# Weights on a second DMA queue, and larger first blocks, in a retention and FFN kernel

## Chip, cores and metric

The kernel runs on one core of one Trainium2 chip. Times are device microseconds (us) of one execution. The kernel before took 227.93 us (median of 3 runs, 227.45 to 228.94). The profiles show one execution each, and their span is some 2 us shorter than the run's time.

Ratios are the mean time of one kernel's fast runs over that of the other's fast runs of the same rounds on the same chip, so they are not quite the ratio of the medians that are quoted beside them. Their intervals are 95% intervals.

## The reference

```python
B, H, S, D = 4, 8, 768, 64                      # q, k, v: float32
gamma = 1.0 - 2.0 ** (-5.0 - np.arange(H))
state = zeros((B, H, D, D))
for t in range(S):                              # retention: linear attention with a decay
    state = gamma * state + einsum('bhd,bhe->bhde', k[:, :, t], v[:, :, t])
    y[:, :, t] = 1/sqrt(D) * einsum('bhd,bhde->bhe', q[:, :, t], state)
x = y.transpose(0, 2, 1, 3).reshape(3072, 512)
h = np.maximum(x @ w_in, 0.0)                   # w_in 512 x 2048
out = h * h @ w_out                             # w_out 2048 x 512
```

## The kernel before

The 3072 tokens are cut into 24 chunks of 128. For each chunk the kernel loads keys, queries and values (256 KB each), casts them, flips keys and queries on TensorE (the timeline's matmuls against `ident`), and does the attention of the chunk in "visits" (the small 64x64 matmuls). The FFN follows: product 1 (`F1`, with `w_in`), relu on ScalarE, square on VectorE, product 2 (`F2`, with `w_out`). Matmuls are in bf16; all inputs come as float32 and are cast on the chip by VectorE, ScalarE or GpSimd.

A list scheduler in Python fixes the order of every engine's instructions when the program is built. It uses assumed durations (the constants below). At run time each engine works through its list strictly in order; semaphores only make it wait.

Loads come in three kinds. The first chunks' keys and queries come as *pairs*: two chunks in one load, in rows of 4 KB. Other chunks, and all values, come in rows of 256 bytes. The weights come in eight loads of 1 MB in rows of 2 KB: `w_in` quarters 0 to 3, `w_out` quarters 0 to 3. Everything is issued by SyncE, on one queue, in the order of `ORDER` (p a pair, i and o quarters of `w_in` and `w_out`).

```python
SMALL = (1.20, 1.55, 65)       # us of queue time assumed for a chunk's load
PAIR = (1.4, 1.6, 9)
WIDE = (2.75, 2.75, 33)        # a quarter of a weight
BLOCKS = [1, 1, 2, 2, 2, 4, 4, 4, 4]   # chunks that share one pass of product 1
WARM = 10.0                    # until then idle time of TensorE is filled with dummy matmuls ("fillers")
NFP = 3                        # pairs
ORDER = "p0 i0 p1 i1 i2 i3 o0 p2 o1 o2 o3"
# ... cut ...
# a pair of keys or queries, and a chunk's values:
nc.sync.dma_start(ld[x][:, slot : slot + 2, :].rearrange("s u n -> s (u n)"),
                  src[x][b : b + 2, :, i * C : (i + 1) * C, :].rearrange("b h (w t) d -> (b h) w (t d)", t=16))
nc.sync.dma_start(t.rearrange("s (h d) -> s h d", h=H),
                  src[x][b, :, i * C : (i + 1) * C, :].rearrange("h s d -> s h d"))
# ... cut ...
def weights(kind, j):
    slot = (j if kind == "in" else 4 + j) % NWS          # one of NWS staging buffers
    # ...
    pl.add(f"ldw{kind}{j}", "SP", WIDE, (), (f"wst{slot}",),
           lambda: nc.sync.dma_start(st[:], wv), prio=dma_prio[(kind, j)])
    for c in range(4):   # casts, by whichever engine the scheduler picks
        pl.add(f"cw{kind}{j}.{c}", WCAST, 0, (f"wst{slot}",), (f"w{kind}{j}.{c}",), ...)
# ... cut ...
def ffn1(blk):
    n = blocks[blk] * C          # 128, 256 or 512 columns
    reads = [f"xt{g % NXT}.{u0 + u}" for u in range(blocks[blk])] + ...   # all chunks of the block
    # 16 feature blocks x 4 matmuls of 128 x n, then relu (ScalarE) and square (VectorE)
```

A block of n chunks costs 64 matmuls of 128·n columns in product 1, and it can start only when all its n chunks are through the attention.

Of the kernel before, what the change touches and what calls it, by code (L numbers as in the profile page):

```python
# [18 lines left out]
class Plan:  # L19
# [6 lines left out]
    DMA_LATENCY = 1.9  # L26
    LAND = 1.25
    RING = 198
    FETCH = 2.6
    BLOCK0 = 193  # L30
    BLOCK = 256
# [32 lines left out]
    def schedule(self, nbanks, max_open):  # L64
        ops = self.ops
        n = len(ops)
        users = [[] for _ in range(n)]
        left = [len(o["deps"]) for o in ops]
        for o in ops:
            for d in o["deps"]:  # L70
                users[d].append(o["i"])
        ready_at = [0.0] * n
        start = [None] * n
        end = [None] * n
        eng_free = {}
        pool = {}
        for o in ops:
            for e in o["eng"]:
                eng_free.setdefault(e, 0.0)
                pool.setdefault(e, set())  # L80
                if left[o["i"]] == 0:
                    pool[e].add(o["i"])
        bank_free = [0.0] * (nbanks - 1) + [WARM]
        bank_of = {}
        open_groups = set()
        shared = [0.0, 0.0]
        outstanding = {e: [] for e in eng_free}
        done = 0
        issued, edge, next_fetched, history, crossed = 0, self.BLOCK0, 3.0, [], 0.0
        while done < n:  # L90
            best = None
            for eng, cand in pool.items():
                ef = eng_free[eng]
                for i in cand:
                    o = ops[i]
                    t = max(ef, ready_at[i])
                    b = o["bank"]
                    if b is not None and b[0] == "open":
                        if b[2] and len(open_groups) >= max_open:
                            continue  # L100
                        free = [x for x in bank_free if x is not None]
                        if not free:
                            continue
                        t = max(t, min(free))
                    key = (t, o["prio"], i)
                    if best is None or key < best[0]:
                        best = (key, i, eng)
            assert best is not None, "no operation can be placed"
            (t, _, _), i, eng = best
            o = ops[i]  # L110
            for e in o["eng"]:
                pool[e].discard(i)
            o["on"] = eng
            dur = o["eng"][eng]
            move = isinstance(dur, tuple)
            if move:
                out_ = outstanding[eng]
                while out_ and out_[0][0] <= t:
                    out_.pop(0)
                while sum(x[1] for x in out_) + dur[2] > self.RING:  # L120
                    t = max(t, out_.pop(0)[0])
            start[i] = t
            b = o["bank"]
            if b is not None and b[0] == "open":
                k = min((x, j) for j, x in enumerate(bank_free) if x is not None)[1]
                bank_free[k] = None
                bank_of[b[1]] = k
                if b[2]:
                    open_groups.add(b[1])
            if move:  # L130
                dur, n_desc = (dur[:2] if t < 50 else dur[:1] * 2), dur[2]
                eng_free[eng] = t + 0.08
                for w in range(2):
                    shared[w] = max(shared[w], t + self.DMA_LATENCY) + dur[w]
                end[i] = max(shared) + self.LAND
                out_.append((max(shared), n_desc))
                dur = 0.08
            else:
                if eng == "PE":
                    o["fill"] = 0  # L140
                    if t < WARM:
                        o["fill"] = int(max(0.0, t - max(eng_free[eng], 1.5) - 0.3) * FILL / 0.213)
                    issued += 2 * o["fill"]
                    todo, per = 2 * o["count"], dur / max(1, 2 * o["count"])
                    now = t
                    while issued + todo > edge:
                        step = max(0, edge - issued)
                        now = max(now + step * per, next_fetched)
                        issued, todo = max(issued, edge), todo - step
                        ahead = next((y for x, y in reversed(history) if x <= edge - self.AHEAD), 0.0)  # L150
                        ahead = max(ahead, crossed)
                        crossed = now
                        edge += self.BLOCK
                        next_fetched = ahead + min(5.7, max(0.3, max(shared) - ahead)) + self.FETCH
                    issued += todo
                    dur = now + todo * per - t
                    history.append((issued, t + dur))
                    o["dur"] = dur
                eng_free[eng] = t + dur
                end[i] = t + dur + o["lat"]  # L160
            if b is not None and b[0] == "close":
                bank_free[bank_of[b[1]]] = end[i]
                open_groups.discard(b[1])
            if b is not None:
                o["bank_index"] = bank_of[b[1]]
            done += 1
            for u in users[i]:
                same = list(ops[u]["eng"]) == [eng] and not move
                ready_at[u] = max(ready_at[u], start[i] + dur if same else end[i] + self.HOP)
                left[u] -= 1  # L170
                if left[u] == 0:
                    for e in ops[u]["eng"]:
                        pool[e].add(u)
        self.start, self.end, self.on = start, end, [o["on"] for o in ops]
        return sorted(range(n), key=lambda i: (start[i], i))


SMALL = (1.20, 1.55, 65)
PAIR = (1.4, 1.6, 9)
WIDE = (2.75, 2.75, 33)  # L180
STORE = (0.72, 0.72, 9)
BLOCKS = [1, 1, 2, 2, 2, 4, 4, 4, 4]
SPLIT = 6
WARM = 10.0
FILL = 0.8
PACE = 6
LEAD = 7
NFP = 3
F2LAG = 5.0
F2WAIT = 4  # L190
CAST = {"k": {"DVE": 0.43, "ACT": 0.63, "POOL": 0.78}, "q": {"DVE": 0.43, "ACT": 0.63, "POOL": 0.78}}
# [2 lines left out]
WPRIO = {"in": -2.0, "out": 2.0}  # L194


ORDER = "p0 i0 p1 i1 i2 i3 o0 p2 o1 o2 o3"


def dma_order(nm):  # L200
# [13 lines left out]
def kernel(  # L214
# [9 lines left out]
    nc = tc.nc  # L224
    P = nc.NUM_PARTITIONS
# [14 lines left out]

    blocks = BLOCKS
    assert sum(blocks) == NM
    NB = len(blocks)
    blk0 = [sum(blocks[:i]) for i in range(NB)]
    for x, n in zip(blk0, blocks):
        assert 512 % (n * C) == 0 and x // 4 == (x + n - 1) // 4
    NLD, NBF, NQT, NXT, NH2, NWS, NOSB, NST = 4, 4, 4, 4, 3, 4, 3, 4
    NBANK = 4

    const = ctx.enter_context(tc.tile_pool(name="const", bufs=1))  # L250
# [5 lines left out]
    ident = sb("ident", [P, P], BF16)  # L256
# [17 lines left out]
    wst = [sb(f"wst{j}", [P, 4, 512], FP32) for j in range(NWS)]  # L274
# [5 lines left out]
    fps = [psum.tile([P, 512], FP32, name=f"fps{j}") for j in range(NBANK)]  # L280
# [3 lines left out]
    pl = Plan()  # L284
# [63 lines left out]
    def prepare(m):  # L348
        b, i = where(m)
        slot = m % NLD  # L350
        for x in "kqv":
            t = ld[x][:, slot, :]
            if x != "v" and m < 2 * NFP:
                if m % 2 == 0:
                    pl.add(f"ld{x}{m}", "SP", PAIR, (), (f"ld{x}{slot}", f"ld{x}{slot + 1}"),
                           lambda x=x: nc.sync.dma_start(  # L356
# [206 lines left out]
    def weights(kind, j):  # L563
        slot = (j if kind == "in" else 4 + j) % NWS
        st = wst[slot]
        dst = w_in_bf[j] if kind == "in" else w_out_bf[j]
        wv = (moe_w_in.rearrange("(cb p) f -> p cb f", p=P)[:, :, j * 512 : (j + 1) * 512] if kind == "in"
              else moe_w_out.rearrange("(fb p) n -> p fb n", p=P)[:, 4 * j : 4 * j + 4, :])
        pl.add(f"ldw{kind}{j}", "SP", WIDE, (), (f"wst{slot}",),
               lambda: nc.sync.dma_start(st[:], wv), prio=dma_prio[(kind, j)])  # L570
        for c in range(4):
            pl.add(f"cw{kind}{j}.{c}", WCAST, 0, (f"wst{slot}",), (f"w{kind}{j}.{c}",),
                   lambda on, c=c: copy_on(on, dst[:, c, :], st[:, c, :]),
                   prio=WPRIO[kind] + j)
# [71 lines left out]
    dma_prio = {x: n for n, x in enumerate(dma_order(NM))}  # L646
# [6 lines left out]
    for m in range(-1, NM):  # L653
# [18 lines left out]
        else:  # L672
            if n == SPLIT:
                transpose(n)
            t = n + 1 if n + 1 < NM else None
# [13 lines left out]
    if tc is not None:  # L689
        with tc.manual_schedule():  # L690
            for i in sequence:
                o = pl.ops[i]
                for _ in range(o.get("fill", 0)):
                    nc.tensor.matmul(fps[NBANK - 1][:, 0 : 2 * P], lhsT=ident[:],
                                     rhs=ident[:, None, :].to_broadcast([P, 2, P]), start=True, stop=True)
                o["fn"](o["on"]) if o["flex"] else o["fn"]()
    return pl

# [29 lines left out]
```

## Time and profile before

| what | number | where it is read |
|---|---|---|
| span, mean granted TensorE clock | 224.9 us, 1.000 | cores |
| TensorE busy from 0 to 40 us | 28.4 of 40 | busy time by stretch |
| TensorE busy from 40 to 90 us | 48.0 of 50 | busy time by stretch |
| TensorE busy from 90 to 221 us | 130.9 of 131 | busy time by stretch |
| first matmul of product 1 | 15.93 us | timeline |

So TensorE is full from about 41 us on, and before that it waits for its inputs. These are lines of the first page of the kernel before: the busy tenths of TensorE, its granted clock and the DMA rate in 40 slices of 5.6 us, and the chain of work that ended last.

```profile
PE   5667878889999998999999999999999999999993
PEclk9999999999999999999999999999999999999999
GB/s 138 246 272 291 382 304 187 366 258 210 273 212 192 226 209 185 234 211 202 203 239 197 51 50 3 47 50 23 24 47 50 47 47 1 47 50 47 93 49 91
...
PE 78%; DMA 11%; SPq 5%; issue 2%; ACT 2%; DVE 1%; POOL 1%; ACTq 0%; POOLq 0%
```

TensorE is 50% to 80% busy in its first slices and then full. The clock row reads 9 throughout, but for its first four slices it is not to be trusted: the trace has no clock record before 23.4 us, and the matmuls show half the pace until then (below). The last chain spends 16% of the span in loads (DMA) and in SyncE's queue (SPq), nearly all of it in the start.

The timeline of TensorE and of SyncE's issues in the kernel before, with start, duration, engine, line, operation and, in brackets, the idle time ahead and what ended it:

```profile
9.54 0.61 PE L422 MATMUL fps<-ident,qkT 128*128 128x128 bf16 x4
15.93 1.33 PE L594 MATMUL fps<-xt,w_in 128*128 128x128 bf16 x11 [1.22 <-DVE xt L556]
25.30 2.13 PE L594 MATMUL fps<-xt,w_in 128*128 128x128 bf16 x31 [0.73 <-DVE w_in L343]
...
2.09 1.21 SPq L363 DMA_DIRECT2D vn<-in_v_dram  x2
3.34 4.84 SPq L570 DMA_DIRECT2D wst<-in_moe_w_in_dram  x1
8.22 0.55 SPq L356 DMA_DIRECT2D kn<-in_k_dram  x1
```

The first pair's keys are flipped back at 9.5 us, and product 1 of chunk 0 starts at 15.9 us. Counted from the starts of the matmuls, those of 128 columns follow one another every 106 to 107 ns before 23.4 us and every 56 ns after it.

### The profile page before, as it was taken

Reading aid. Unit: us, or ns where it says so; the run is one execution under the profiler, and the core shown is the slowest. Engines: PE = TensorE matmul, PEld = TensorE weight load, DVE = VectorE, ACT = ScalarE, POOL = GpSimd, SP = SyncE. Lnnn points to the kernel's source line nnn. Section 1 sums busy time; section 2 is a strip of 40 time slices with the busy share of each in tenths; the row PEclk is TensorE's granted clock in tenths of the full one; section 3 lists DMA queues with packets and bytes.
Section 4 is the critical chain, followed back from the end, with each engine's and each line's share of the span. In section 5 each row is a group of like instructions: output and inputs, shape, how many; then the busy total and the mean of one; then the engine's idle time right before and its main releaser. Section 6 shows DMA issues by size and latency. Waiting matters only on the chain.

```text
span 224.9 us, 7277 instructions
## 1 busy us (share of the span) xinstructions
PE 207.4 (92%) x3242; PEld 118.3 (53%) x3242; DVE 116.0 (52%) x251; ACT 105.4 (47%) x167; POOL 40.1 (18%) x65
## 2 busy tenths in 40 slices
PE   5667878889999998999999999999999999999993
PEld 3547766744577874455555554444444444444441
DVE  1496878772189985899887754422222222230000
ACT  8233626853357763576545564344435444343121
POOL 3221225234233322324323100000000000000000
PEclk9999999999999999999999999999999999999999
DMA  6999999999999998999998110110011110111212
GB/s 138 246 272 291 382 304 187 366 258 210 273 212 192 226 209 185 234 211 202 203 239 197 51 50 3 47 50 23 24 47 50 47 47 1 47 50 47 93 49 91
DMA packets 70975, 34.02 MB, mean 151 GB/s; under 512 B 63008, under 2 KB 63008, under 8 KB 70944
## 3 DMA queue, kind: packets, MB, share of 16 engines
q1 hardware_dynamic: 70944, 33.56, 59.3%
q8 instruction: 25, 0.41, 0.8%
q14 instruction: 6, 0.05, 0.1%
HBM read 27.26 MB, written 6.29 MB: 149 GB/s over the span
## 4 chain that ended last, share of the span: by engine, by line
PE 78%; DMA 11%; SPq 5%; issue 2%; ACT 2%; DVE 1%; POOL 1%; ACTq 0%; POOLq 0%
PE fps L632 35%; PE fps L594 33%; DMA qn<-in_q_dram 11%; PE yy L390 3%; SPq L570 2%; SPq L356 2%; PE yy L469 2%; PE sc L480 1%; ACT qkT L437 1%; PE yy L454 1%; PE sc L491 1%; DVE xt L556 1%; POOL qs L345 1%; SPq L363 1%; PE yy L403 0%
## 5 line engine op out<-in xcount | busy, mean ns | idle before, releaser
L594 PE MATMUL fps<-xt,w_in 128*128 128x512 bf16 (+2 forms) x576 | 96.9, 313 | 2.2 <-DVE xt L556 1.2
L632 PE MATMUL fps<-w_out,h 128*128 128x512 bf16 x384 | 92.9, 379 | 0.0
L599 ACT ACTIVATE h<-fps 128x512 bf16<-128x512 f32 x96 | 57.1, 596 | 58.2 <-PE fps L594 58.1
L604 DVE TENSOR_TENSOR h<-h 128x512 bf16<-128x512 bf16 x96 | 44.3, 476 | 49.9 <-ACT h L599 49.8
L594 PEld LDWEIGHTS <-w_in 128*128 128x128 bf16 x576 | 51.1, 100 | 34.3 <-issue 1.8
L632 PEld LDWEIGHTS <-h 128*128 128x128 bf16 x384 | 36.9, 98 | 43.3
L640 ACT ACTIVATE osb<-fps 128x512 f32<-128x512 f32 x24 | 14.3, 597 | 26.9 <-PE fps L632 26.9
L556 DVE TENSOR_TENSOR xt<-yy,yf 128x512 bf16<-128x512 f32 x24 | 16.5, 689 | 18.8 <-ACT qkT L437 16.2
L437 ACT ACTIVATE qkT<-yy 128x1024 bf16<-128x1024 bf16 x18 | 18.4, 1024 | 11.5 <-PE yy L469 10.3
L345 POOL CAST ks<-kn 128x512 bf16<-128x512 f32 x21 | 15.2, 725 | 35.8 <-DMA kn<-in_k_dram 25.0
L378 DVE TENSOR_TENSOR vs<-vn,vf 128x512 bf16<-128x512 f32 x24 | 17.8, 741 | 4.9 <-DMA vn<-in_v_dram 4.9
L345 POOL CAST qs<-qn 128x512 bf16<-128x512 f32 x21 | 14.1, 673 | 22.8 <-DMA qn<-in_q_dram 22.6
L547 DVE TENSOR_TENSOR state<-sc,state 128x256 bf16<-128x256 f32 x40 | 16.7, 418 | 0.5
L534 DVE TENSOR_TENSOR pt<-sc,cmask 128x512 bf16<-128x512 f32 x24 | 16.3, 681 | 0.8 <-PE sc L491 0.8
L469 PE MATMUL yy<-qkT,state 64*64 64x64 bf16 x352 | 12.3, 200 | 0.4
L454 PE MATMUL yy<-pt,vs 64*64 64x64 bf16 x384 | 7.8, 198 | 2.2 <-issue 1.4
L480 PE MATMUL sc<-qkT 64*64 64x64 bf16 x384 | 8.2, 198 | 1.5 <-issue 1.5
L469 PEld LDWEIGHTS <-state 64*64 64x64 bf16 x352 | 7.6, 107 | 1.2 <-PE yy L469 1.2
L491 PE MATMUL sc<-vs,ks 64*64 64x64 bf16 x352 | 7.7, 197 | 0.0
L454 PEld LDWEIGHTS <-vs 64*64 64x64 bf16 x384 | 5.5, 110 | 3.9 <-issue 2.8
L345 POOL CAST w_out<-wst 128x512 bf16<-128x512 f32 x7 | 5.3, 781 | 11.7 <-DMA wst<-in_moe_w_out_dram 11.7
L390 PEld LDWEIGHTS <-ks 64*64 64x64 bf16 x288 | 3.7, 107 | 6.8 <-issue 6.6
(46 smaller groups left out, 87.4 us busy)
## 6 DMA issues: line engine op xcount, KB each, us to landing
vn<-in_v_dram SPq DMA_DIRECT2D x24, 256.0 KB, 5.5
out_dram<-osb SPq DMA_DIRECT2D x24, 256.0 KB, 2.0
kn<-in_k_dram SPq DMA_DIRECT2D x18, 256.0 KB, 5.2
qn<-in_q_dram SPq DMA_DIRECT2D x18, 256.0 KB, 5.4
wst<-in_moe_w_in_dram SPq DMA_DIRECT2D x4, 1024.0 KB, 10.8
wst<-in_moe_w_out_dram SPq DMA_DIRECT2D x4, 1024.0 KB, 13.0
kn<-in_k_dram SPq DMA_DIRECT2D x3, 512.0 KB, 8.0
qn<-in_q_dram SPq DMA_DIRECT2D x3, 512.0 KB, 10.1
```

What stands on the lines that cost most here:

```text
L345: nc.gpsimd.tensor_copy(o, t)
L378: lambda: nc.vector.tensor_tensor(out=o[:], in0=t.rearrange("s (h d) -> s h d", h=H), in1=vf[:, i, :, None].to_broadcast([P, H, D]), op=AL ...
L437: lambda: nc.scalar.activation(qkT.rearrange("p x j (s t) -> p s (x j) t", s=2), tpv.rearrange("p s (g t) -> p s g t", t=L), AF.Copy), pri ...
L454: nc.tensor.matmul(yy[L * c : L * c + L, sub, p * L : p * L + L], lhsT=vs[r, 4 * a + j, :], rhs=pt[r, a, j, :], start=(p == 0), stop=True, ...
L469: nc.tensor.matmul(yy[L * c : L * c + L, sub, p * L : p * L + L], lhsT=st[r, j, :], rhs=qkT[r, 1, j, sub * L : sub * L + L], start=False, ...
L534: lambda: nc.vector.tensor_tensor(out=pt[:], in0=sc[:, :, 0:256].rearrange("s g (p t) -> s g p t", p=NJ), in1=cmask[:, None, None, :].to_b ...
L547: f = lambda cc=cc, j1=j1, j0=j0: nc.vector.tensor_tensor(out=sts[j1][:], in0=cc, in1=sts[j0][:], op=ALU.add)
L556: lambda: nc.vector.tensor_tensor(out=xt[:, :, u * C : u * C + C].rearrange("s p (g t) -> s g p t", g=2), in0=yy[:, :, 0:256].rearrange("s ...
L594: nc.tensor.matmul(ps[:, u * n : u * n + n], lhsT=w_in_bf[j][:, cb, c * P : (c + 1) * P], rhs=xt[:, cb, cols], start=(cb == 0), stop=(cb = ...
L599: nc.scalar.activation(h2[:, f0 : f0 + per, cols], ps[:].rearrange("p (u n) -> p u n", u=per), AF.Relu)
L604: nc.vector.tensor_mul(hv, hv, hv)
L632: nc.tensor.matmul(ps[:], lhsT=h2[:, fb, u * C : u * C + C], rhs=w_out_bf[j][:, c, :], start=(fb == 0), stop=(fb == NFB - 1))
```

## The change

The intent is to let weights and chunks load side by side, so that more bytes are moved early, and to save matmuls of product 1 with larger first blocks. The core of the diff:

```diff
+    MIX = {"SP": 1.25, "ACT": 1.8}       # how much slower each queue is assumed to run beside the other
@@ the scheduler's model of the loads: one shared clock becomes one per queue
-                for w in range(2):
-                    shared[w] = max(shared[w], t + self.DMA_LATENCY) + dur[w]
+                mine, other = shared[eng], max(shared[e] for e in shared if e != eng)
+                begin, slow = max(mine, t + self.DMA_LATENCY), self.MIX[eng]
+                both = max(0.0, min(other - begin, dur[1] * slow))
+                shared[eng] = begin + both + max(0.0, dur[1] - both / slow)
@@ constants
-PAIR = (1.4, 1.6, 9)
+PAIR = (2.4, 2.4, 9)
-BLOCKS = [1, 1, 2, 2, 2, 4, 4, 4, 4]
-SPLIT = 6
-WARM = 10.0
+BLOCKS = [2, 2, 4, 4, 4, 4, 4]
+SPLIT = 4
+WARM = 20.0
-LEAD = 7
-NFP = 3
+LEAD = 5
+NFP = 2
-ORDER = "p0 i0 p1 i1 i2 i3 o0 p2 o1 o2 o3"
+ORDER = "p0 p1 i0 i1 i2 i3 o0 o1 o2 o3"
@@ staging buffers of the weights: NWS 4 -> 3; fillers of 512 columns in place of 256
@@ weights
-        pl.add(f"ldw{kind}{j}", "SP", WIDE, (), (f"wst{slot}",),
-               lambda: nc.sync.dma_start(st[:], wv), prio=dma_prio[(kind, j)])
+        pl.add(f"ldw{kind}{j}", "ACT", WIDE, (), (f"wst{slot}",),
+               lambda: nc.scalar.dma_start(st[:], wv), prio=-150 + dma_prio[(kind, j)])
```

More of the change, by code (lines that the diff above doesn't have):

```diff
@@ L85, in schedule @@
         open_groups = set()
-        shared = [0.0, 0.0]
+        shared = {"SP": 0.0, "ACT": 0.0}
         outstanding = {e: [] for e in eng_free}
@@ L132, in schedule @@
                 eng_free[eng] = t + 0.08
-                for w in range(2):
-                    shared[w] = max(shared[w], t + self.DMA_LATENCY) + dur[w]
-                end[i] = max(shared) + self.LAND
-                out_.append((max(shared), n_desc))
+                mine, other = shared[eng], max(shared[e] for e in shared if e != eng)
+                begin, slow = max(mine, t + self.DMA_LATENCY), self.MIX[eng]
+                both = max(0.0, min(other - begin, dur[1] * slow))
+                shared[eng] = begin + both + max(0.0, dur[1] - both / slow)
+                end[i] = shared[eng] + self.LAND
+                out_.append((shared[eng], n_desc))
                 dur = 0.08
@@ L141, in schedule @@
                     if t < WARM:
-                        o["fill"] = int(max(0.0, t - max(eng_free[eng], 1.5) - 0.3) * FILL / 0.213)
+                        o["fill"] = int(max(0.0, t - max(eng_free[eng], 1.5) - 0.3) * FILL / 0.427)
                     issued += 2 * o["fill"]
@@ L153, in schedule @@
                         edge += self.BLOCK
-                        next_fetched = ahead + min(5.7, max(0.3, max(shared) - ahead)) + self.FETCH
+                        next_fetched = ahead + min(5.7, max(0.3, max(shared.values()) - ahead)) + self.FETCH
                     issued += todo
@@ L246 @@
         assert 512 % (n * C) == 0 and x // 4 == (x + n - 1) // 4
-    NLD, NBF, NQT, NXT, NH2, NWS, NOSB, NST = 4, 4, 4, 4, 3, 4, 3, 4
+    NLD, NBF, NQT, NXT, NH2, NWS, NOSB, NST = 4, 4, 4, 4, 3, 3, 3, 4
     NBANK = 4
@@ L693 @@
                 for _ in range(o.get("fill", 0)):
-                    nc.tensor.matmul(fps[NBANK - 1][:, 0 : 2 * P], lhsT=ident[:],
-                                     rhs=ident[:, None, :].to_broadcast([P, 2, P]), start=True, stop=True)
+                    nc.tensor.matmul(fps[NBANK - 1][:], lhsT=ident[:],
+                                     rhs=ident[:, None, :].to_broadcast([P, 4, P]), start=True, stop=True)
                 o["fn"](o["on"]) if o["flex"] else o["fn"]()
```

## The prediction

> **What bounds the kernel now.** Two regimes. From 90 to 221 us TensorE is busy 130.9 of 131 us (busy time by stretch). From 40 to 90 us it is busy 48.0 of 50. Before 41 us it lacks inputs: the chain of waits runs through loads (DMA of q 11% of the span, SyncE's queue 5%). The timeline shows the one queue's order: first key pair usable at 6.4 us, its values 10.6, w_in quarter 0 at 14.1, second pair's q 18.9, third pair's q 37.8, and the last quarter of w_out at 50.0. TensorE's first FFN matmul starts at 15.9. Rates over 2 us stretches: weights 384 to 399 GB/s, 4 KB pairs and 256-byte rows only 170 to 250.
>
> **What changes.**
> 1. Weights go on ScalarE's queue. The Trainium skill ("DMA: Bandwidth & Descriptors", "Issuing engines are not separate DMA queues") says that both share 16 engines and only issue time is saved; this trace, with one load queue, cannot show it. As pairs and chunks draw half the weights' rate, I expect the mixture to move more (estimate 300 to 350 GB/s against 10.2 MB in the first 39.4 us, 259 GB/s, now). Chunk loads then run about a quarter slower than alone, weights nearly twice as slow. Estimate: w_out complete at 42 to 46 us (was 50), chunks 4 to 7 landed at 45 to 50 (was 56.8).
> 2. One pair less: some 2 us more queue time, hidden.
> 3. Blocks. The matmul count of the first product drops from 576 to 448. From the timeline, 128 columns cost 77 ns, 256 cost 115, 512 cost 216: 128x77 + 192x115 + 256x216 = 87.2 us becomes 128x115 + 320x216 = 83.8 us, so 3.4 us less TensorE work. But the first FFN matmul waits for two chunks and, by the order of instructions, for the flips of the second pair: it starts later, near 20 us (15.9 before).
> 4. ScalarE gives about 0.55 us (SyncE's figure) to each of eight issues: small.
> 5. Fillers: 16 of 512 instead of 18 of 256 columns: little.
>
> **Sum.** Dense TensorE work left from the point where it is no longer starved, which by the new order is the arrival of chunk 7, about 46 us: 16x115 ns + 320x216 + 376x216 of the FFN, 17 visits of 0.93 = 168 us, plus 1.5 us of stalls and 3.65 us of tail: span about 219. The same sum for before (178 us from 41.0, plus 2.2) gives the observed 221.3. Median runs are 3 us over the profiled span.
>
> **Prediction: 221 us**, 8 in 10 between 213 and 229. Faster by over 2%: 0.62; within 2%: 0.29; slower: 0.09.
>
> **What shows it right or wrong.** Stretches: 0 to 40 us moves 300 GB/s or more (step 1), w_out lands before 46. First FFN matmul near 20 us, and TensorE dense from about 46 us with at most 2 us idle afterwards. In the chain the share of DMA falls.
>
> **What would make it wrong.** If mixing gives no more bytes, chunk 7 lands near 57 us as now, and the time is 229 or more. If the weights' 2 KB rows crowd out the values' 256-byte rows, the first visits slip past 17 us. "Issue" pauses of TensorE (three of 0.8 to 1.4 us before 48 us now) could grow with two full queues. If mixing is better than I estimate, dense work starts by 40 us and the time nears 214.

## The result

The changed kernel takes 236.05 us (median of 4, 234.89 to 236.58) beside 227.82 us (median of 4) of the kernel before in the same rounds: a ratio of 1.0346, interval 1.029 to 1.0402. It is 3.5% slower. Executions over 1.5% slower than the fastest of the same kernel are left out of the means. The prediction was 221 us.

The same lines of the changed kernel's page; a slice is 5.9 us here:

```profile
PE   5205879489999999999999999999999999999993
PEclk9655559859999999999999999999999999999998
GB/s 215 261 337 221 333 341 311 268 207 226 177 204 207 202 197 170 182 223 215 181 243 92 47 0 47 47 47 0 47 45 46 20 28 45 45 45 47 89 45 89
...
PE 76%; DMA 18%; issue 1%; SPq 1%; ACT 1%; POOL 1%; DVE 0%; POOLq 0%; ACTq 0%
```

The third slice of TensorE is 0: it does nothing in these 5.9 us, which lie within a wait of 9.1 us (below). By the trace's clock records its clock had fallen to half before that, at 7.8 us, in a first idle time of 4.1 us. It stays there until 35.1 us, and falls once more from 45.4 to 52.2 us. In the kernel before the half pace ended at 23.4 us. The Trainium skill ("TensorE: Matmul & The Clock Gate", "Part 1: The HAM clock gate") says that an idle TensorE drops to half its clock and that busy time brings it back. This trace agrees: eight matmuls of 256 columns take 1.89 us at 32.3 us, where the clock row reads 5, and 1.05 us at 43.9 us. The loads' share of the last chain rose from 11% to 18%. The rate row shows that the change did move more bytes early (mean of 0 to 40 us, by stretches: 262 GB/s before, 288 after), which was its intent.

How much of product 1 was done by when? Busy time of the lines of product 1 alone, by stretch: start and end, length, TensorE busy and number of matmuls, weight loads of TensorE, and for all engines together the clock, the DMA share and GB/s. First the kernel before, then the changed one:

```profile
0.00:40.00 40.00, 12.57 (x152) 10.90 (x152) 1.00 1.02 262
40.00:50.00 10.00, 4.70 (x40) 3.77 (x40) 1.00 1.02 323
```

```profile
0.00:40.00 40.00, 5.87 (x41) 4.20 (x42) 0.66 1.04 288
40.00:50.00 10.00, 2.94 (x24) 2.16 (x24) 0.77 1.05 252
```

Until 50 us the changed kernel has done 65 matmuls of 256 columns, which is one chunk pair's 64 and one more. The kernel before has done 192 matmuls, 128 of 128 columns and 64 of 256: four chunks. The loss is there: after 50 us TensorE is busy for another 178.3 us in the changed kernel and for 170.2 us in the kernel before, and these 8.1 us are most of the 9.9 us between the two spans. Later the two kernels work alike: from 90 us to its last matmul TensorE is idle for 0.1 us in the kernel before and for 1.0 us in the changed one.

Why did the start slip? The timelines of the changed kernel, first TensorE, then ScalarE, then SyncE's issues:

```profile
9.16 1.11 PE L406 MATMUL sc<-ident,ks 128*64 128x64 bf16 x32 [4.08 <-DVE ks L346]
10.21 0.61 PE L697 MATMUL fps<-ident 128*128 128x512 bf16 x1
19.91 1.03 PE L425 MATMUL fps<-ident,qkT 128*128 128x128 bf16 x8 [9.10 <-ACT qkT L344]
...
32.34 1.89 PE L597 MATMUL fps<-xt,w_in 128*128 128x256 bf16 x8
...
7.65 1.15 ACT L344 ACTIVATE w_in<-wst 128x512 bf16<-128x512 f32 x2 [0.50 <-DMA wst<-in_moe_w_in_dram]
18.84 0.37 ACTq L573 DMA_DIRECT2D wst<-in_moe_w_in_dram  x1
19.26 0.60 ACT L344 ACTIVATE qkT<-sc 128x512 bf16<-128x512 f32 x1 [10.46 <-DMA vn<-in_v_dram]
...
2.09 3.90 SPq L366 DMA_DIRECT2D vn<-in_v_dram  x2
6.03 7.49 SPq L359 DMA_DIRECT2D kn<-in_k_dram  x1
```

The keys of the first pair are flipped at 9.2 to 10.3 us. Half of the result waits on ScalarE for its evacuation from PSUM (`qkT<-sc`), and ScalarE does this only at 19.26 us. Ahead of it in ScalarE's list stands the issue of the fourth weight load. That issue itself takes 0.37 us, but it started at 18.84. The bracket says what ended the idle time: the landing of a *value* load, which is SyncE's and has nothing to do with the weights. TensorE stood for 9.1 us. Even then product 1 started only at 32.3 us, since the second pair and the values had come late as well.

When did the loads land? Counted from the landing events of the trace, in us:

```
                    pair 0: k    q     v0     v1  | pair 1: k    q     v2     v3 | w_in0 w_in3 w_out3
before                   6.4   8.5   9.6   10.7  |        16.3  18.9  19.8   20.9 | 14.1  29.7  50.0
after                    8.7  11.7  17.5   18.7  |        21.0  23.2  24.4   25.5 |  7.6  29.6  45.4
```

The values of the first pair came 8 us later than before. The last of the weights came 4.6 us earlier. The weights won, the chunks lost.

### How the two queues shared the engines

This table is counted from the DMA records of the changed kernel's trace. q1 is SyncE's queue, q10 ScalarE's; "rows" are the records of one size that ended in the 2 us stretch, on all 16 DMA engines; the last column of each queue is the mean time of one row.

```
stretch      q1, 256-byte rows             q10, 2 KB rows
12 to 14 us   321 rows,  41 GB/s, 19 ns     306 rows, 313 GB/s, 93 ns
30 to 32 us   322 rows,  41 GB/s, 19 ns     308 rows, 315 GB/s, 93 ns
48 to 50 us  1644 rows, 210 GB/s, 20 ns     none
22 to 24 us, kernel before (one queue)      368 rows, 377 GB/s, 88 ns
```

The numbers of rows are nearly equal. Equal numbers would also come of longer turns of equal length, so the order of the records was looked at (they don't name the engine). From 12 to 14 us each 256-byte row has on average 1.15 ends of 2 KB rows 4 or 5 ns after its start, where chance gives 0.3. Each 2 KB row has 1.25 ends of 256-byte rows 3 or 4 ns after its start. Ends of other 256-byte rows are no more frequent there than chance, as they would be in longer turns. So, while both queues have work, the engines take one row of each in turn, whatever its size, and in this pair of sizes a row takes about as long as it would alone. So a 256-byte row waits for a 2 KB row each time: these loads run at a fifth of their own rate (41 of 210 GB/s), while the weights lose only a sixth (315 of 377). From the times of the rows alone one would expect, for 2304 bytes on 16 engines, 2304·16/(19 + 88 ns) = 345 GB/s; the sum measured is 356. For these two sizes sharing neither adds nor loses a rate; it only gives the time to the large rows. The 4 KB rows of the pairs are the larger ones and fare better: 170 to 176 GB/s beside the weights (6 to 10 us), some 235 alone (18 to 22 us), and it is the weights that fall, to 81 to 93 GB/s. The counts are again alike (83 rows beside 79, 86 beside 91), but here a 2 KB row takes 140 ns and not 88.

The Trainium skill ("DMA: Bandwidth & Descriptors", "Issuing engines are not separate DMA queues") says that DMAs interleave on the same 16 engines whoever starts them. The trace agrees, as far as the row times of the 256-byte and 2 KB rows add. The same page ("Queues, rings and completion order", "Arbitration") says that an engine drains a whole packet, typically about 9 to 17 descriptors, from one ring before it switches. The counts and the order here do not show that for these loads: they show single rows in turn. Whether each row was a packet of its own is not shown.

### The profile page after: what moved, and what is told of

Its sections match the earlier page's. It is cut to its first block, busy times and chain, and to the rows that moved or that the text cites. A ratio compares the mean times of both kernels' runs of the same rounds, so it can differ in the third digit from the quotient of the medians.

```text
span 234.8 us, 6986 instructions
## 1 busy us (share of the span) xinstructions
PE 207.1 (88%) x3079; PEld 109.9 (47%) x3104; DVE 110.4 (47%) x246; ACT 107.8 (46%) x168; POOL 38.2 (16%) x65
## 3 DMA queue, kind: packets, MB, share of 16 engines
q1 hardware_dynamic: 70592, 25.17, 45.4%
## 4 chain that ended last, share of the span: by engine, by line
PE 76%; DMA 18%; issue 1%; SPq 1%; ACT 1%; POOL 1%; DVE 0%; POOLq 0%; ACTq 0%
PE fps L635 35%; PE fps L597 33%; DMA kn<-in_k_dram 8%; DMA vn<-in_v_dram 6%; DMA qn<-in_q_dram 4%; PE yy L393 3%; PE yy L472 1%; PE yy L457 1%; PE sc L494 1%; PE sc L483 1%; SPq L359 1%; ACT qkT L440 0%; POOL qs L348 0%; DVE xt L559 0%; SPq L366 0%
## 5 line engine op out<-in xcount | busy, mean ns | idle before, releaser
L597 PE MATMUL fps<-xt,w_in 128*128 128x512 bf16 (+1 forms) x440 | 96.2, 352 | 0.6 <-issue 0.2
L635 PE MATMUL fps<-w_out,h 128*128 128x512 bf16 x367 | 94.2, 384 | 1.4 <-issue 0.7
L607 DVE TENSOR_TENSOR h<-h 128x512 bf16<-128x512 bf16 x96 | 41.2, 439 | 60.5 <-ACT h L602 60.1
L597 PEld LDWEIGHTS <-w_in 128*128 128x128 bf16 x448 | 43.4, 99 | 39.3 <-issue 0.9
L440 ACT ACTIVATE qkT<-yy 128x1024 bf16<-128x1024 bf16 x20 | 20.5, 1024 | 11.5 <-PE yy L472 9.3
L559 DVE TENSOR_TENSOR xt<-yy,yf 128x512 bf16<-128x512 f32 x24 | 16.6, 690 | 17.0 <-ACT qkT L440 15.6
L348 POOL CAST ks<-kn 128x512 bf16<-128x512 f32 x21 | 13.9, 662 | 51.2 <-DMA kn<-in_k_dram 26.1
L381 DVE TENSOR_TENSOR vs<-vn,vf 128x512 bf16<-128x512 f32 x24 | 16.7, 694 | 5.0 <-DMA vn<-in_v_dram 4.9
L472 PE MATMUL yy<-qkT,state 64*64 64x64 bf16 x352 | 12.4, 202 | 0.3
L425 PE MATMUL fps<-ident,qkT 128*128 128x128 bf16 x16 | 2.1, 312 | 9.1 <-ACT qkT L344 9.1
L697 PE MATMUL fps<-ident 128*128 128x512 bf16 x16 | 7.2, 587 | 1.6 <-POOL ident L300 1.6
L393 PE MATMUL yy<-ident,qs 64*64 64x64 bf16 x320 | 6.3, 195 | 2.3 <-POOL qs L348 1.8
```

What stands on the lines that cost most here:

```text
L348: nc.gpsimd.tensor_copy(o, t)
L381: lambda: nc.vector.tensor_tensor(out=o[:], in0=t.rearrange("s (h d) -> s h d", h=H), in1=vf[:, i, :, None].to_broadcast([P, H, D]), op=AL ...
L393: nc.tensor.transpose(tpv[L * a : L * a + L, sub, 256 * x + j * L : 256 * x + j * L + L], bf[name][m % NBF][r, j, a, :], ident[r, r])
L440: lambda: nc.scalar.activation(qkT.rearrange("p x j (s t) -> p s (x j) t", s=2), tpv.rearrange("p s (g t) -> p s g t", t=L), AF.Copy), pri ...
L472: nc.tensor.matmul(yy[L * c : L * c + L, sub, p * L : p * L + L], lhsT=st[r, j, :], rhs=qkT[r, 1, j, sub * L : sub * L + L], start=False, ...
L559: lambda: nc.vector.tensor_tensor(out=xt[:, :, u * C : u * C + C].rearrange("s p (g t) -> s g p t", g=2), in0=yy[:, :, 0:256].rearrange("s ...
```

## The experiments

There were three theories. In the expectations they go by letters:

- **A, crowding.** The small rows of the chunks are starved beside the weights' larger rows, so the attention starts late.
- **B, blocks.** The larger blocks make product 1 wait for more chunks.
- **C, standing in line.** ScalarE has to issue weight loads in the midst of its computing. An issue can wait for something else, and all that stands behind it waits too.

On C the trace says more. The landing events fall on eight counters that are used in turn by the loads of *both* queues. In the changed kernel the counter that served the value load v1 (complete at 18.74 us) is the one that next served `w_in` quarter 3 (complete at 29.60 us), and that quarter was issued at 18.84. The issue waited until its counter was free. It could also have waited for its staging buffer, but the four casts that read the buffer had ended by 8.8 us. In gated and free_scalar the trace's record of an issue itself names the counter that it waits for: in gated the issue at 24.48 us waits for counter 103, which a query load of SyncE's queue completed at 24.46 us.

"k/after" in a heading means that the edit was made to the changed kernel, "k/before" to the kernel before. All results were correct.

### Undoing one part, and doing one part alone

**one_queue** (k/after): weights back on SyncE's queue, all else as changed.

```diff
-        pl.add(f"ldw{kind}{j}", "ACT", WIDE, ..., lambda: nc.scalar.dma_start(st[:], wv), prio=-150 + dma_prio[(kind, j)])
+        pl.add(f"ldw{kind}{j}", "SP", WIDE, ..., lambda: nc.sync.dma_start(st[:], wv), prio=dma_prio[(kind, j)])
```

> The changed kernel with the eight weight loads put back on SyncE's queue (same blocks, pairs, fillers). Theory A (sharing the DMA engines row by row with the 2 KB weight rows starves the 256-byte rows): values of the first pair land near 10.7 us again (18.7 in the changed kernel), TensorE's first FFN matmul near 21 us, total within 2% of before (0.98 to 1.01). Rival B (the blocks, the pairs or the fillers cost the time): the total stays near 1.03.

Measured: 233.81 us, ratio to before 1.0254 (1.0192 to 1.0316). The first pair lands as in the kernel before (6.4, 8.7, 9.9 and 11.6 us at the latest), product 1 starts at 21.86 us, and yet the kernel is 2.5% slower. So the queue is not all of it; this was a miss. The interval also overlaps the changed kernel's (1.029 to 1.0402), so it is not settled that taking out the queue alone gained anything there.

**two_queues_only** (k/before): only the weights moved to ScalarE's queue, and nothing else.

```diff
-        pl.add(f"ldw{kind}{j}", "SP", WIDE, ..., lambda: nc.sync.dma_start(st[:], wv), prio=dma_prio[(kind, j)])
+        pl.add(f"ldw{kind}{j}", "ACT", WIDE, ..., lambda: nc.scalar.dma_start(st[:], wv), prio=-150 + dma_prio[(kind, j)])
```

> The kernel before with only the weight loads moved to ScalarE's queue (old blocks, three pairs, four staging buffers). Theory A: slower than before by 2 to 6%, values of the first pair landing at 19 us or later, since four weight quarters can be in flight. Rival B: within 1% of before.

Measured: 237.48 us, ratio 1.0433 (1.0381 to 1.0484). The second queue alone costs at least as much as the whole change, and the ratio lies inside the band of A. The values of the first pair landed at 18.5 and 21.7 us. Its largest wait of TensorE, with the total, the number of times and the longest, is the known one:

```profile
PE fps L422 <- ACT qkT L341: 9.7, 1, 9.7
```

**blocks_only** (k/before): `BLOCKS = [2, 2, 4, 4, 4, 4, 4]` and nothing else.

> The kernel before with only the blocks changed to two of two chunks, then four. Theory: TensorE's work falls by about 3 us but the first FFN matmul comes later (near 21 us instead of 15.9), so the total is 0.985 to 1.01 of before. If the blocks were the cause of the loss: 1.02 or more.

Measured: 232.48 us, ratio 1.0221 (1.0164 to 1.0277). The expectation of 0.985 to 1.01 missed, and the other one, that the blocks cost time, held. The loss sits in one stretch. Busy time of each engine (TensorE first, then its weight loads, VectorE, ScalarE, GpSimd) with the clock at the end, in the kernel before, then in blocks_only:

```profile
60.00:70.00 10.00, 9.88 (x255) 7.67 (x244) 7.03 (x14) 5.54 (x9) 3.03 (x4) 1.00 0.99 210
```

```profile
60.00:70.00 10.00, 5.08 (x215) 3.50 (x207) 5.38 (x11) 3.67 (x4) 1.84 (x3) 0.76 1.01 230
```

From 60 to 70 us TensorE is half idle. It has finished the products of the first four chunks, and the next block takes four whole chunks of attention, so its first 512-column matmul comes at 70.65 us. In the kernel before there are two blocks of two chunks in between. On one queue B is a real part. The prediction put the end of TensorE's starving at the arrival of chunk 7, and its sum has no idle time for the block of four.

**blocks_twos** (k/before): `BLOCKS = [2, 2, 2, 2, 4, 4, 4, 4]`, the same saving at the start without the early block of four.

> The kernel before with blocks of two chunks four times, then four chunks. Blocks of 2, 2, 4 alone cost 2.2%, with TensorE idle for 5 us between 60 and 70 us before the first block of four. If that wait for four whole chunks was the cost, then here it goes and the total is 0.985 to 1.005 of before. If the lack of one-chunk blocks at the start was the cost, it stays at 1.015 to 1.025.

Measured: 224.91 us, ratio 0.9919 (0.9883 to 0.9955), 0.8% faster than before. TensorE is busy 9.94 us of the 10 from 60 to 70. This confirms the reading of blocks_only.

**after_twos** (k/after): the same blocks in the changed kernel.

> The changed kernel with blocks 2, 2, 2, 2, then 4. With one queue this change of blocks was worth 3% (1.022 to 0.992). In the changed kernel TensorE was dense from 48.9 us on, the second product of the first four chunks came late enough to bridge the wait for chunks 4 to 7; so here it should be worth little: within 1% of the changed kernel's 1.035 (1.025 to 1.045). If blocks cost here as they do on one queue, it falls to 1.01 or less.

Measured: 236.68 us, ratio 1.0429 (1.0359 to 1.0499). The intervals of this and of the changed kernel overlap. With two queues no gain from the smaller blocks can be seen; that the start is so late that they no longer matter is the likely reason, and not shown.

So the parts do not add: the blocks alone 1.022, the queue alone 1.043, and the change with both (and with one pair less, other fillers and one staging buffer less) 1.035.

**twos_warm** (blocks_twos with the change's fillers): `WARM = 20`, 512 columns.

> The 2, 2, 2, 2, 4 kernel on one queue with the change's fillers (512 columns, placed up to 20 us of the plan instead of 10). If they keep TensorE at its full pace from the first FFN matmul, the first 8 matmuls of 256 columns take 0.95 us instead of 1.89 and the time falls by 1 to 2 us (0.983 to 0.99). If not: within 0.5% of 0.992.

Measured: 225.82 us, ratio 0.9932 (0.9883 to 0.998), against 0.9919 without. The fillers are worth nothing that these runs can show.

### The size of the weights' rows

**rows_1k** (k/after): each weight load split in two of half the columns, so rows of 1 KB.

```diff
-               lambda: nc.scalar.dma_start(st[:], wv), ...
+               lambda: [nc.scalar.dma_start(st[:, :, x : x + 256], wv[:, :, x : x + 256]) for x in (0, 256)], ...
```

> The changed kernel with each weight load split into two of 256 columns (1 KB rows instead of 2 KB). If the DMA engines take one row of each queue in turn, then beside the weights the 256-byte rows get about 60 to 65 GB/s (40 with 2 KB rows) and the weights about 240 to 260 GB/s (315), a ratio of bytes of 1 to 4 instead of 1 to 8. If they share by bytes, the two rates stay as they were. The time itself is not the question of this run.

One look, with one time, 241.3 us (state unknown, so not compared). Counted from the DMA records:

```
stretch      q1, 256-byte rows             q10, 1 KB rows
12 to 14 us   490 rows,  63 GB/s, 19 ns     486 rows, 249 GB/s, 55 ns
14 to 16 us   491 rows,  63 GB/s, 19 ns     482 rows, 247 GB/s, 55 ns
```

Rows in turn again, at equal counts. The 256-byte rows now get 63 GB/s in place of 41. That is the number that one row in turn gives.

**pool_queue** (k/after): weights issued by GpSimd on its own queue; GpSimd no longer casts.

```diff
-        pl.add(f"ldw{kind}{j}", "ACT", WIDE, ..., lambda: nc.scalar.dma_start(st[:], wv), ...)
+        pl.add(f"ldw{kind}{j}", "POOL", WIDE, ..., lambda: nc.gpsimd.dma_start(st[:], wv), ...)
-CAST = {"k": {"DVE": 0.43, "ACT": 0.63, "POOL": 0.78}, "q": {"DVE": 0.43, "ACT": 0.63, "POOL": 0.78}}
+CAST = {"k": {"DVE": 0.43, "ACT": 0.63}, "q": {"DVE": 0.43, "ACT": 0.63}}      (and WCAST alike)
```

> The changed kernel with the weight loads issued by GpSimd on its own queue, GpSimd freed of casts (ScalarE and VectorE take them). No engine's computing stands behind an issue any more, and the completion counters are no longer shared with the chunk loads, but there are still two queues on the same DMA engines. Theory A (rows alternate one for one, so 256-byte rows beside 2 KB rows get about 40 GB/s): values of the first pair still land at 17 us or later, TensorE still waits for chunks 4 and 5, total 1.01 to 1.04 of before. Theory C (ScalarE standing behind issues that wait for another queue's loads): the long pauses of TensorE go, total 1.00 or less.

Measured: 237.91 us, ratio 1.0504 (1.0466 to 1.0542), slower than A's band of 1.01 to 1.04 too. This run is the strongest for A. ScalarE issues no load here, and TensorE's wait for the flip's evacuation (`fps L425 <- ACT qkT L344`) falls from 9.1 us to 0.9:

```profile
PE fps L425 <- ACT qkT L344: 0.9, 1, 0.9
```

The two queues also have eight counters each here, and share none. Yet product 1 starts at 31.34 us (32.34 in the changed kernel) and the kernel is as slow all the same, so C cannot be the only cause. The crowding is harder here: the records of this queue are 4 KB (from 12 to 14 us: 167 of them, 342 GB/s, 179 ns, against 183 rows of 256 bytes at 23 GB/s), and v1 landed at 23.6 us. A third size of row, and again one in turn. The run is not pure: the fillers, which wait for a table that GpSimd makes, began at 4.4 us rather than 1.6.

### Taking ScalarE's standing away

Four runs tried to remove C alone. None did so cleanly, but each shows what the standing costs.

**unblocked** (k/after): in ScalarE's order the issues of `w_in` 3 and `w_out` 0, and the casts behind them, are put after the first pair's evacuations.

```diff
+    sequence = put_after(("ldwin3", "ldwout0"), ("Ek1", "G0", "G1", "Eq0", "Eq1"))
+    sequence = put_after(("cwin2.0", "cwin2.1", "cwin2.2", "cwin2.3"), ("ldwout0",))
+    sequence = put_after(("ldwout1",), ("cq2", "cq3"))
+    sequence = put_after(("cwin3.0", "cwin3.1", "cwin3.2", "cwin3.3", "ldwout2"), ("Eq2", "Eq3", "G2"))
```

> The changed kernel with ScalarE's own order changed: the evacuations and casts of the first two pairs stand before the weight issues and weight casts that they stood behind. Theory A1 (what binds is the arrival of chunks 4 and 5 past 46 us): the 9.1 us pause of TensorE goes or moves, the first FFN matmul comes 4 to 8 us earlier (24 to 28 us instead of 32.3), but TensorE waits for the loads of chunk 5 until about 47 us all the same, and the total moves by less than 1% (1.025 to 1.035 of before). Rival C (ScalarE standing in order behind a weight issue costs the time): the total falls by 6 to 9 us, to 0.995 to 1.01 of before.

Measured: 243.74 us, ratio 1.0717 (1.0656 to 1.0778), the slowest run that was timed in rounds. Both theories' numbers missed. The timeline of ScalarE shows why, and the last line is from TensorE's waits:

```profile
36.09 0.40 ACTq L573 DMA_DIRECT2D wst<-in_moe_w_out_dram  x1
36.53 0.60 ACT L602 ACTIVATE h<-fps 128x512 bf16<-128x512 f32 x1 [0.52 <-issue]
48.72 0.38 ACTq L573 DMA_DIRECT2D wst<-in_moe_w_out_dram  x1
49.14 1.08 ACT L602 ACTIVATE h<-fps 128x512 bf16<-128x512 f32 x2 [12.01 <-DMA qn<-in_q_dram]
...
PE yy L457 <- DVE pt L537: 12.7, 3, 12.2
```

TensorE's first wait for the flip's evacuation is down to 0.9 us, but ScalarE stands elsewhere, and product 1 still starts at 31.97 us. Then another standing of 12 us comes: the issue of the last weight load waited for a query load of chunk 6 on the other queue, which landed at 48.62 us on the counter that had its turn. TensorE was idle for 12.2 us in that time. Its wait names VectorE (`pt`) as the releaser; that ScalarE's standing lies behind it is read from the times, which agree, and was not tested by itself.

**fewer_loads** (k/after): the values of each pair in one load, so two loads fewer ahead.

> The changed kernel with the values of each of the two pairs in one load instead of two, so that two loads fewer take completion counters early. The fourth w_in quarter then waits for the second quarter (13.8 us) instead of the first pair's last values (18.7 us). Theory C: TensorE's 9.1 us pause shrinks to 4 us or so, and the total falls by 4 to 6 us to 1.01 to 1.02 of before. Theory A: the fourth quarter is in flight sooner and takes the row slots of the second pair, whose loads land 2 to 4 us later; total within 1% of the changed kernel (1.025 to 1.045).

Measured: 237.05 us, ratio 1.0473 (1.0421 to 1.0525). The old wait shrank to 3.9 us, as C said, but the time did not fall to C's 1.01 to 1.02, and it lies a little above A's band (1.025 to 1.045). Two new waits came, and product 1 started only at 39.4 us. TensorE's waits:

```profile
PE yy L414 <- ACT qs L344: 7.1, 1, 7.1
PE yy L465 <- DVE pt L545: 5.2, 1, 5.2
PE fps L433 <- ACT qkT L344: 3.9, 1, 3.9
```

**gated** (k/after): ScalarE reads one element of the first pair's cast values before it issues any weight, so the first pair loads alone.

```diff
+                pl.add("gate", "ACT", 0.1, ("bfv0", "bfv1"), ("gate",), lambda: nc.scalar.activation(
+                    gate[:], bf["v"][1][:, 0, 0:1], AF.Copy), prio=-150)
-        pl.add(f"ldw{kind}{j}", "ACT", WIDE, (), (f"wst{slot}",),
+        pl.add(f"ldw{kind}{j}", "ACT", WIDE, ("gate",), (f"wst{slot}",),
@@ the calls that add the weight loads to the plan are moved behind the gate
```

> The changed kernel, still two queues, but ScalarE reads one element of the first pair's cast values before it issues the first weight load, so the first pair has the DMA engines to itself. Theory A: its values land near 10.7 us as on one queue (18.7 in the changed kernel) and TensorE's first FFN matmul comes at 20 to 27 us instead of 32.3; the later chunks are still crowded while weights flow, to about 55 us, so the total stays above one queue's (1.025) or near it: 1.02 to 1.05 of before.

Measured: 237.51 us, ratio 1.0462 (1.0396 to 1.0528). The first pair lands as on one queue (6.3, 8.5, 9.1, 9.9 us), and still nothing is gained, for the second pair is crowded in its stead and ScalarE stands at its issues:

```profile
15.64 9.30 ACTq L574 DMA_DIRECT2D wst<-in_moe_w_in_dram  x2
24.99 0.63 ACT L345 ACTIVATE qs<-qn 128x512 bf16<-128x512 f32 x1 [12.40 <-DMA qn<-in_q_dram]
...
25.67 0.64 PE L407 MATMUL yy<-ident,qs 128*64 128x64 bf16 x16 [6.05 <-ACT qs L345]
```

ScalarE was idle for 12.4 us and TensorE for 6.0 us behind it. Product 1 started at 28.0 us, a little past the 20 to 27 that A gave; the time lies in A's band. The 12.4 us cover two issues.

**free_scalar** (k/after): ScalarE has no casts and no evacuations at the start, it makes its tables (`yf`) before it issues weights, there are five staging buffers in place of three, and the plan knows the measured sharing (256-byte rows 5.2 times slower, pairs 1.4, weights 1.2).

```diff
-                begin, slow = max(mine, t + self.DMA_LATENCY), self.MIX[eng]
+                begin = max(mine, t + self.DMA_LATENCY)
+                slow = 1.2 if eng == "ACT" else 5.2 if n_desc == 65 else 1.4
-CAST = {"k": {"DVE": 0.43, "ACT": 0.63, "POOL": 0.78}, ...      (ACT taken out of CAST, WCAST and EVAC)
+CAST = {"k": {"DVE": 0.43, "POOL": 0.78}, ...
-    NLD, NBF, NQT, NXT, NH2, NWS, NOSB, NST = 4, 4, 4, 4, 3, 3, 3, 4
+    NLD, NBF, NQT, NXT, NH2, NWS, NOSB, NST = 4, 4, 4, 4, 3, 5, 3, 4
-        pl.add(f"ldw{kind}{j}", "ACT", WIDE, (), (f"wst{slot}",),
+        pl.add(f"ldw{kind}{j}", "ACT", WIDE, ("yf",), (f"wst{slot}",),
```

> The changed kernel with ScalarE freed of casts and of the first evacuations (VectorE and GpSimd take them), its tables first, then the weight issues, with five staging buffers, and the plan's sharing of the DMA engines set to what was measured. Nothing that the first chunks need stands behind an issue. Theory C: the total falls to 1.01 of before or less. Theory A: beside the weights the 256-byte rows still get about 40 GB/s, chunk 5 still lands past 44 us, and the total stays at 1.02 to 1.04.

Measured: 239.1 us, ratio 1.0546 (1.0456 to 1.0636). Product 1 now starts at 25.88 us, the earliest of the two-queue versions, and then its relu, which only ScalarE does, stands behind the issues:

```profile
32.25 4.20 ACTq L574 DMA_DIRECT2D wst<-in_moe_w_out_dram  x3
36.50 0.60 ACT L603 ACTIVATE h<-fps 128x512 bf16<-128x512 f32 x1 [30.79 <-POOL w_in L349]
...
PE fps L598 <- ACT h L603: 9.0, 2, 7.1
```

C as the sole cause (a time near the kernel before's) falls, as it did with pool_queue. A's band (1.02 to 1.04) was passed too; C had come back in another place, which may be why.

**mix_measured** (k/after): only the plan's sharing as in free_scalar.

> The changed kernel with one constant of its plan replaced: a 256-byte-row load beside weights is planned 5.2 times as long as alone (was 1.25), a pair 1.4 times, a weight load 1.2 times (was 1.8). Only the fixed order of instructions follows from it. If the loss came mostly from an order built on wrong arrival times (theory C), the total falls to 1.015 of before or less; if from the arrivals themselves (theory A), it stays at 1.025 to 1.05.

Measured: 238.07 us, ratio 1.0482 (1.04 to 1.0565). A rival that remained, that the order was merely built on wrong durations, falls: built on the measured ones it is no faster.

### A version that beats both

**twos_halves** (blocks_twos, one queue): each pair's load of keys or queries as two loads of 2 KB rows in place of one of 4 KB rows.

```diff
-                           lambda x=x: nc.sync.dma_start(
-                               ld[x][:, slot : slot + 2, :].rearrange("s u n -> s (u n)"),
+                           lambda x=x: [nc.sync.dma_start(
+                               ld[x][:, slot + u, :],
                                 src[x][b : b + 2, :, i * C : (i + 1) * C, :].rearrange(
-                                   "b h (w t) d -> (b h) w (t d)", t=16)),
+                                   "b h (w t) d -> (b h) w (t d)", t=16)[:, :, 512 * u : 512 * u + 512])
+                               for u in range(2)],
```

> The 2, 2, 2, 2, 4 kernel on one queue with each 4 KB-row load of keys or queries split into two loads of 2 KB rows. 4 KB rows took about 280 ns each in the trace, 2 KB weight rows about 88: if 2 KB rows of keys are as quick, the first pair lands 2 us sooner, and the time falls by 1 to 3 us to 0.98 to 0.988 of before. If what makes these rows slow is where they lie, not their length, nothing changes (0.99 to 0.995).

Measured: 222.55 us, ratio to before 0.9787 (0.9737 to 0.9838): some 5 us faster than the kernel before and 13 us than the changed one. Whether it is over 2% faster is not settled, as the interval holds 0.98; that it is faster is. The time fell as far as was expected if 2 KB rows were as quick as the weights', but that is not what happened. The halves' rows go no faster than the 4 KB rows did (240 GB/s from 4 to 6 us, against 244 in the kernel before), but the first half is usable at 4.3 us, where the whole pair was at 6.4, and the values follow at 8.9 and 10.0 us. The two stretches of the start, blocks_twos first, then twos_halves:

```profile
0.00:20.00 20.00, 11.45 (x234) 8.24 (x235) 10.06 (x37) 7.88 (x11) 6.15 (x16) 1.00 0.94 214
20.00:40.00 20.00, 18.16 (x332) 14.25 (x333) 15.88 (x36) 11.15 (x21) 5.41 (x8) 1.00 1.06 316
```

```profile
0.00:20.00 20.00, 12.52 (x267) 9.22 (x268) 11.11 (x38) 8.44 (x13) 5.22 (x16) 1.00 0.95 236
20.00:40.00 20.00, 18.91 (x348) 14.83 (x347) 16.85 (x38) 12.16 (x23) 5.56 (x8) 1.00 1.05 326
```

TensorE is busy 1.8 us longer in these 40 us. That is about half of the 3.9 us by which the profiled span is shorter than that of blocks_twos (220.1 and 224.0 us); the rest was not traced. The change sought an earlier start with a second queue; smaller pieces on the one queue gave one, with product 1 at 19.87 us (21.06 in blocks_twos).

## Why the prediction was wrong

The prediction's sum gave a span of about 219 us for the profiled run, and 234.8 was measured. The difference of 15.6 us is found term by term:

| term of the sum | predicted | measured | difference |
|---|---|---|---|
| TensorE no longer starved from | 46 us | about 50 us | +4 |
| TensorE work left from there | 168 us | 178.3 us busy after 50 us | +10.3 |
| idle after that | 1.5 us | 2.6 us | +1.1 |
| tail after the last matmul | 3.65 us | 3.9 us | +0.2 |

The second line is the largest. The sum counted 16 matmuls of 256 columns as left to do in product 1, and 17 visits. At 50 us there were about 63 of those matmuls left (128 less the 65 above) and 19 visits. Part of the rest ran with a cold clock (until 52.2 us).

1. **Step 1, the sharing, failed in its sizes.** It said that chunk loads would run "about a quarter slower than alone, weights nearly twice as slow". Measured: 256-byte rows five times slower (210 to 41 GB/s), weights a sixth slower (377 to 315). These two sizes are those of the change's own plan (`MIX`, 1.25 and 1.8), so it seems that they were taken over from it; the engines share the time row by row. The prediction listed this as its own risk ("the weights' 2 KB rows crowd out the values' 256-byte rows"), with too small a weight.
2. **Step 1, its totals.** More bytes did move (288 GB/s in the first 40 us, under the 300 named), and `w_out` was complete at 45.4 us, inside the 42 to 46. That part was right, and it was worthless: in the waits shown above TensorE stood for chunks and not for weights. The chunks' part was wrong: chunk 7 was to land by 50 us, and its values landed at 54.5 us. Nor did its arrival end the starving, as the sum had it: TensorE was nearly full from 50 us (9.5 of 10 us) with work that had been left undone.
3. **Step 2, one pair less,** was not tried alone; it stays untested.
4. **Step 3, the start of product 1.** It said 20 us, and it was 32.3. About 9 us of TensorE's standing lie in one wait (`fps L425 <- ACT qkT L344`). Step 3 saw that blocks of two wait for two chunks, but gave no cost to a block of four that waits for four. On one queue blocks_only puts that at 2.2% by itself; in the changed kernel after_twos shows no gain from taking it away.
5. **Step 3, the saving of matmuls,** was right in its counts, 576 became 448, but not in its size. Its 77 ns for 128 columns is a mean over the half pace before 23.4 us and the full one after. At the full pace that the trace of the kernel before shows (56, 109 and 216 ns for 128, 256 and 512 columns), 83.4 us become 83.1: 0.3 us saved and not 3.4. blocks_twos came out 0.8% faster, and it is not shown why.
6. **Step 4, ScalarE's issues, failed.** It took 0.55 us for each. An issue does take 0.37 us when it starts. But it can wait first, and ScalarE waits with it: 10.5 us in the changed kernel (the bracket above), 12 in unblocked, and 12.4 over two issues in gated. The Trainium skill's "Rules for kernel authors" in "DMA: Bandwidth & Descriptors" say that spreading loads over engines gives no bandwidth and only saves issue time; the prediction hoped for bandwidth in spite of this. The runs agree on bandwidth, and add a cost.
7. **Step 5, the fillers,** was right: nothing.

So the step that failed first is step 1: its quarter for the chunk loads was a factor of five for the 256-byte rows. Step 4, whose half microsecond became 10.5, failed beside it.

Shown: the small rows are starved row by row (three sizes of rows beside them), the second queue alone costs 4.3% and the blocks alone 2.2% when either is put into the kernel before, and ScalarE's standing is neither the only cause (pool_queue) nor harmless (unblocked, gated, free_scalar).

Left open: how the 4.3% divides between crowding and standing. Every run that took one wait away made another, and with the weights on a computing engine's queue the two could not be parted. That an issue waits for its completion counter is read from the order of landings, from the brackets of the timeline and from the counters that some issues name in the trace; only pool_queue changed the counters (eight for each queue), and it changed more than that, so it is not tested by itself. In the changed kernel itself it is open how much either part costs: the same kernel on one queue (1.025) and with the smaller blocks (1.043) have intervals that overlap its own. Which of the smaller constants (`NWS`, `NFP`, `LEAD`, `SPLIT`) add to the change's loss was not tried one by one; one_queue (1.025) and blocks_only (1.022) agree so closely that little is left for them on one queue.

## What to carry to other kernels

A second DMA queue adds no rate of its own here; it changes who is served, and large rows win against small ones by their ratio of sizes. Here it was best to keep all loads on the one queue, with what is needed first ahead, and to cut the first loads into pieces that can be used sooner. gated, which let the first pair load alone and then used two queues, gained nothing. Be wary of giving loads to the queue of an engine that the critical path needs: an issue stands in that engine's order, and it can wait there for a load of another queue. And check a clock row against the pace of the matmuls: where the trace had no clock record, the row read full while TensorE ran at half pace.

## What the Trainium skill lacked or had wrong

- "DMA: Bandwidth & Descriptors", "Queues, rings and completion order": it says that an engine drains a packet of about 9 to 17 descriptors before it switches queues. For these loads the turns were single rows: 321 rows of 256 bytes beside 306 of 2 KB, 490 beside 486 of 1 KB, 183 beside 167 records of 4 KB, each in 2 us. Whether each row was a packet of its own is not shown. What this does to rates is not said: 41, 63 and 23 GB/s for the 256-byte rows, where they have 210 alone.
- The same page, "Issuing engines are not separate DMA queues" and "Rules for kernel authors": only saved issue time is told of. The runs show a cost: in unblocked ScalarE stood for some 12 us at an issue that takes 0.38 us.
- No page that was read for this tells that an issue on one queue can have to wait for a load of the other because both take their completion counters from one set. Here eight served all loads in turn, and `w_in` 3, on ScalarE's queue, was issued at 18.84 us, just after a value load of SyncE's queue had completed on its counter at 18.74 us. In pool_queue each queue had eight of its own.
- No page that was read explains the rate of the pairs' rows: 4 KB rows of keys and queries ran at about 240 GB/s alone on one queue (283 ns each), and 2 KB rows of the same data at 240 (125 ns), while 2 KB rows of the weights ran at 377 to 397 (86 to 90 ns; kernel before, 10 to 12 and 20 to 30 us).
